# An empty place between the choice of the one-hot clusters and their turning

## The chip, the cores and the metric

The kernel runs on one core of a Trainium2 chip. The metric is the device time of one execution in microseconds. TensorE (PE) multiplies and transposes, VectorE (DVE), ScalarE (ACT) and GpSimd (POOL) do the elementwise work, SyncE (SP) issues most transfers. The four compute engines each run their own instruction stream and meet at semaphores.

## The reference, cut to what matters

```python
q_assign = argmax(einsum('bhsd,hcd->bhsc', q_n, c_n), -1)   # 16 clusters
k_assign = argmax(einsum('bhsd,hcd->bhsc', k_n, c_n), -1)
mask = q_assign[:, :, :, None] == k_assign[:, :, None, :]
scores = where(mask, 0.125 * q @ k.T, -1e9)
x = softmax(scores) @ v          # batch 4, 8 heads, 768 tokens, width 64
# then: 3072 tokens x 512, the best of 8 experts for each token
out[token] = gate * (relu(x[token] @ w1[e]) @ w2[e])        # 512 -> 1024 -> 512
```

Everything is float32. A query attends only to the keys that chose the same of 16 clusters. The change lies in the attention part.

## The kernel before

**Pairs and units.** The work of attention is cut into 16 pairs: a pair is a batch and two neighbouring heads, whose two widths of 64 fill 128 partitions. Inside a pair there are two halves of the queries (384 each), and for each half six blocks of 128 keys. A block for a half is a unit; six units make a group, and a pair has twelve units in two groups. Each unit has three steps. `scores` (L329) multiplies on TensorE: first the one-hot clusters `kH` and `qH` (bf16), which add a large bonus where the clusters match, then `kT` and `qT` into the same PSUM tile `s_ps`. `expo` (L345) takes the exponential on ScalarE into `prob`. `attend` (L350) multiplies `v` with `prob` on TensorE and adds `prob` up in `acc` on VectorE. When a group has ended, `total` (L379) sums `acc` over the keys on TensorE and ScalarE copies it to `den`; `divide` (L394) takes the reciprocal of `den` on VectorE (L400) and multiplies it with the result into `xT` (L401); `rows` (L411) turns `xT` back on TensorE and ScalarE copies it to `xr`.

**Preparation.** While pair n runs, pair n+1 is prepared in nine pieces (`prep_pieces`, L209): three pieces turn q and k (`turn`), `products` multiplies them with the cluster centres, `assign` turns the products and marks the maxima (`sel`), which GpSimd weights (L258), `choose` (L260) makes the one-hot tile `oh` from them on VectorE (L264, L265), `turn_hot(0, "q")` turns the query half of `oh` with six transposes on TensorE (L277) and VectorE copies it to `qH` (L283), `turn_hot(1, "k")` does the same for the keys and ScalarE copies it to `kH` (L285), and `mean` makes a small column `ev` (L298, L306) that `divide` reads. The pieces are kept in the list `prepare`.

**Order.** TensorE, VectorE and ScalarE run the order in which the program is written (`manual_schedule`). The loop at L517 takes two units per turn, so a pair has six turns, here called turn 0 to turn 5. A turn writes, in this order: `scores` and `expo` of the two units that come next, a first piece of preparation, `rows` of the group before (in turns 2 and 5), `attend` of the two present units, `total` and `divide` of the group before (in turns 0 and 3), a second piece of preparation, and a piece of routing if there is one. So a pair has twelve places for pieces, of which nine were used: `assign` and `choose` had the two places of turn 2, the two `turn_hot` those of turn 3, and `mean` the first of turn 4. Fifteen pairs prepare another one; pair 0 itself is prepared ahead of the loop.

**Routing.** After each batch of four pairs, five routing pieces (`route_pieces`, L428) are taken one per turn, from turn 3 of the following pair on: in pairs 4, 8 and 12 `products` (L440) comes in turn 3 and `logits` in turn 4, and in pairs 5, 9 and 13 `choose` (L470) comes in turn 1, with two ScalarE table loads.

**PSUM for the small pieces.** Every preparation piece, `total`, `rows` and the routing pieces take their PSUM tile from `misc()` (L114). Its pool has two buffers, which are handed out by turns:

```python
psM = at.enter_context(tc.tile_pool(name="psM", bufs=2, space=PSUM))
def misc():
    return psM.tile([P, 512], F32, tag="misc", name="misc")
```

The one-hot tiles `oh` (two, L169), `qH` and `kH` (two each) alternate from pair to pair. `prob` has five buffers, `s_ps` two.

Of the kernel before, what the change touches and what calls it, by code (L numbers as in the profile page):

```python
# [35 lines left out]
def kernel(  # L36
# [67 lines left out]
    with ExitStack() as at:  # L104
# [9 lines left out]
        def misc():  # L114
            return psM.tile([P, 512], F32, tag="misc", name="misc")
# [4 lines left out]
        def load(n):  # L120
            b, hp = pairs[n]
            t = ld[n] = {}
            for nm, src in (("q", q), ("k", k), ("v", v)):
                t[nm] = ldp.tile([P, NJ, 2, D], F32, tag=nm + "32", name=nm + "32")
                for h in range(2):
                    nc.sync.dma_start(
                        out=t[nm][:, :, h],
                        in_=src[b, 2 * hp + h].rearrange("(p j) d -> p j d", j=NJ),
                    )
# [79 lines left out]
        def prep_pieces(n):  # L209
# [62 lines left out]
            def turn_hot(i, nm):  # L272
                hot = t[nm + "H"] = trp.tile([P, S], BF16, tag=nm + "H", name=nm + "H")
                bk = misc().bitcast(BF16)
                for j in range(NJ):
                    half, u = divmod(j, NJ // 2)
                    nc.tensor.transpose(  # L277
                        bk[:, P * j : P * j + P],
                        oh[:, u, 2 * i + half].rearrange("p h c -> p (h c)"),
                        identb,  # L280
                    )
                if nm == "q":
                    nc.vector.tensor_scalar(hot, bk[:, 0:S], BIG, None, ALU.mult)  # L283
                else:
                    nc.scalar.copy(hot, bk[:, 0:S])  # L285
# [10 lines left out]
            def mean():  # L296
# [16 lines left out]
                products,  # L313
                assign,
                choose,
                lambda: turn_hot(0, "q"),
                lambda: turn_hot(1, "k"),
                mean,
# [10 lines left out]
        def scores(i):  # L329

            n, hq, j = units[i]
            t = ld[n]
            s_ps = un[i]["s_ps"] = psS.tile([P, 2, 512], F32, tag="s_ps", name="s_ps")
            for l, r, first in (("kH", "qH", True), ("kT", "qT", False)):
                for h in range(2):
                    rows = slice(D * h, D * h + D)
                    nc.tensor.matmul(  # L337
                        s_ps[:, h, 0:HS],
                        lhsT=t[l][rows, P * j : P * j + P],
                        rhs=t[r][rows, HS * hq : HS * hq + HS],  # L340
                        start=first,
                        stop=not first,
                    )

        def expo(i):  # L345
            d = un[i]
            d["prob"] = pp.tile([P, 2, HS], F32, tag="prob", name="prob", bufs=5)
            nc.scalar.activation(d["prob"], d["s_ps"][:, :, 0:HS], ACTF.Exp)  # L348

        def attend(i):  # L350

            n, hq, j = units[i]
            d, g = un[i], gr[i // GU]
            if j == 0:
                g["o_ps"] = psO.tile([P, 512], F32, tag="o_ps", name="o_ps")
            for h in range(2):
                nc.tensor.matmul(  # L357
                    g["o_ps"][D * h : D * h + D, 0:HS],
                    lhsT=ld[n]["v"][:, j, h],
                    rhs=d["prob"][:, h],  # L360
                    start=(j == 0),
                    stop=(j == NJ - 1),
                )
            if j == 1:
                g["acc"] = pp.tile([P, 2, HS], F32, tag="acc", name="acc")
                nc.vector.scalar_tensor_tensor(
                    out=g["acc"],
                    in0=un[i - 1]["prob"],
                    scalar=NJ * EPS,
                    in1=d["prob"],  # L370
                    op0=ALU.add,
                    op1=ALU.add,
                )
                un[i - 1].clear()
            elif j > 1:
                nc.vector.tensor_tensor(g["acc"], g["acc"], d["prob"], ALU.add)  # L376
                d.clear()

        def total(g):  # L379

            d = gr[g]
            bk = misc()
            for h in range(2):
                nc.tensor.matmul(  # L384
                    bk[D * h : D * h + D, 0:HS],
                    lhsT=ones,
                    rhs=d["acc"][:, h],
                    start=True,
                    stop=True,
                )  # L390
            d["den"] = smp.tile([P, HS], F32, tag="den", name="den")
            nc.scalar.copy(d["den"], bk[:, 0:HS])  # L392

        def divide(g):  # L394
            n, hq, _ = units[GU * g]
            b, hp = pairs[n]
            d = gr[g]
            if (b, hq) not in xT:
                xT[b, hq] = xp.tile([P, NHP, HS], F32, tag="xT", name="xT", bufs=3)
            nc.vector.reciprocal(d["den"], d["den"])  # L400
            nc.vector.scalar_tensor_tensor(  # L401
                out=xT[b, hq][:, hp],
                in0=d["o_ps"][:, 0:HS],
                scalar=ld[n]["ev"],
                in1=d["den"],
                op0=ALU.add,
                op1=ALU.mult,
            )
            d.clear()

        def rows(g):  # L411

            n, hq, _ = units[GU * g]
            b, hp = pairs[n]
            U = NJ // 2
            bk = misc()
            for u in range(U):
                nc.tensor.transpose(  # L418
                    bk[:, P * u : P * u + P], xT[b, hq][:, hp, P * u : P * u + P], ident
                )  # L420
            if b not in xr:
                xr[b] = xp.tile([P, NJ, XW], F32, tag="xr", name="xr")
            nc.scalar.copy(
                xr[b][:, U * hq : U * hq + U, P * hp : P * hp + P],
                bk[:, 0:HS].rearrange("p (u w) -> p u w", w=P),
            )
# [78 lines left out]


        prepare, routing = [], []
        with tc.manual_schedule(engines={EngineType.PE, EngineType.DVE, EngineType.Activation}):
            for piece in prep_pieces(0):
                if piece:  # L510
                    piece()
            for m in range(2):
                scores(m)
                expo(m)


            for i in range(0, len(units) + 6, 2):  # L517
                g, part = divmod(i, GU)
                if i < len(units) and i % (2 * NJ) == 0:
                    n = i // (2 * NJ)  # L520
                    assert not prepare
                    if n + 1 < len(pairs):
                        load(n + 1)
                        prepare = prep_pieces(n + 1)
                    if n == 1:

                        for w in range(2):
                            nc.sync.dma_start(
                                out=w1s[w], in_=moe_w1[0].rearrange("(c p) f -> p c f", p=P)
                            )  # L530
                            nc.sync.dma_start(
                                out=w2s[w], in_=moe_w2[0].rearrange("(c p) d -> p c d", p=P)
                            )
                for m in range(i + 2, min(i + 4, len(units))):
                    scores(m)
                    expo(m)
                if prepare:
                    prepare.pop(0)()
                if part == 4 and g > 0:
                    rows(g - 1)  # L540
                for m in range(i, min(i + 2, len(units))):
                    attend(m)
                if part == 0 and g > 0:
                    total(g - 1)
                    divide(g - 1)
                if prepare:
                    prepare.pop(0)()
                if routing:
                    routing.pop(0)()
                if part == 4 and g > 0 and g % (2 * NHP) == 0:  # L550
                    assert not routing
                    routing = route_pieces(g // (2 * NHP) - 1)
            for piece in routing:
                piece()
# [250 lines left out]
```

## Time and profile before

| | |
|---|---|
| median of 3 runs | 924.09 us (923.74 to 926.51) |
| the profiled execution's own time | 926.38 us |
| its span, first to last instruction | 924.4 us |
| busy in the span: PE, DVE, ACT, POOL | 847.7, 358.7, 302.8, 127.9 us |
| mean granted TensorE clock | 0.966 of full speed |

Times in the profile count from the start of the span. The attention part lasts to about 480 us, the routing to about 500 us, and the experts take the rest. A line of the timeline gives the start, the duration, the engine, the line of the kernel, the operation, the output tile and its inputs, and how many instructions were merged; in brackets stands how long the engine sat idle before it and what ended that. The ends of matmuls are modelled, so the distance from one start to the next is the better measure of what a step on TensorE costs. In the rows by stretch the engines stand in the order PE, PEld (the weight loads), DVE, ACT, POOL, each with its number of instructions.

### The profile page before, as it was taken

The page shows a single profiled execution, that of the slowest core. Times are in us where ns is not written, and L with a number is a line of the kernel's source. Part 1 is how long each engine was busy: PE and PEld are TensorE (multiplying, and loading weights), DVE is VectorE, ACT ScalarE, POOL GpSimd, SP SyncE. Part 2 cuts the span into 40 slices and gives each one's busy share as a digit, 9 for nine tenths or more (in the row PEclk, how much of TensorE's full clock was granted, in tenths as well). Part 3 has the DMA queues.
Part 4 walks back from the last instruction along what each step waited for, and adds up shares of the span by engine and source line. Part 5 has one row for each costly group of instructions (what it writes and reads, how often), then busy time and mean ns, then how long its engine had stood idle before and what let it go on. Part 6 is the DMA issues. An engine that isn't in the chain of part 4 may idle for free.

```text
span 924.4 us, 12733 instructions
## 1 busy us (share of the span) xinstructions
PE 847.7 (92%) x5207; PEld 497.6 (54%) x5207; DVE 358.7 (39%) x488; ACT 302.8 (33%) x485; POOL 127.9 (14%) x171
## 2 busy tenths in 40 slices
PE   4999999899998999989943999999999999999996
PEld 2444444344444444434413777676776767677672
DVE  3577676777767777676754000000000000000000
ACT  3445555545455455555540111111111111111110
POOL 4011010211111110111003001111010111101010
PEclk8999999999998999999965999999999999999998
DMA  9822211322203222010002173374746566514610
GB/s 245 291 53 52 52 34 34 106 52 52 49 21 103 52 52 52 19 69 18 1 0 103 41 275 135 122 301 146 283 171 257 200 227 243 199 36 166 256 35 20
DMA packets 105645, 106.85 MB, mean 116 GB/s; under 512 B 77157, under 2 KB 77157, under 8 KB 105072
## 3 DMA queue, kind: packets, MB, share of 16 engines
q1 hardware_dynamic: 100928, 92.30, 31.0%
q0 software_dynamic: 4480, 13.65, 3.9%
q8 instruction: 43, 0.70, 0.3%
q14 instruction: 18, 0.15, 0.0%
q10 hardware_dynamic: 176, 0.05, 0.0%
HBM read 152.11 MB, written 13.64 MB: 179 GB/s over the span
## 4 chain that ended last, share of the span: by engine, by line
PE 39%; issue 28%; DMA 19%; DVE 10%; ACT 2%; POOL 1%; SPq 0%; POOLq 0%; DVEq 0%
DMA out_dram<-y,sidx 18%; PE s_ps L337 15%; PE o_ps L357 13%; DVE acc L376 4%; PE misc L220 3%; PE misc L384 2%; PE misc L235 2%; PE misc L277 2%; DVE oh L265 1%; PE misc L418 1%; DVE sel L257 1%; DVE amax L256 1%; PE misc L440 1%; DVE pm L264 1%; PE misc L248 1%
## 5 line engine op out<-in xcount | busy, mean ns | idle before, releaser
L709 PEld LDWEIGHTS h_ps<-xTm,w1s 128*128 128x128 f32 x1792 | 204.2, 193 | 21.4 <-DVE xTm L699 19.0
L709 PE MATMUL h_ps<-xTm,w1s 128*128 128x128 f32 x1792 | 208.2, 277 | 2.3 <-DMA w1s<-in_moe_w_dram 2.3
L722 PE MATMUL y_ps<-w2s,hT 128*128 128x512 f32 x448 | 201.2, 592 | 0.0
L348 ACT ACTIVATE prob<-s_ps 128x768 f32<-128x768 f32 x192 | 153.4, 811 | 89.9 <-PE s_ps L337 67.7
L699 DVE COPY xTm<-x_ps 128x512 f32<-128x512 f32 x28 | 19.4, 691 | 379.7 <-PE x_ps L697 379.7
L337 PE MATMUL s_ps<-qT,kT 64*128 64x384 f32 x768 | 157.6, 489 | 0.0
L357 PE MATMUL o_ps<-prob,v 128*64 128x384 f32 x768 | 148.9, 510 | 0.0
L376 DVE TENSOR_TENSOR acc<-acc,prob 128x768 f32<-128x768 f32 x128 | 130.2, 1017 | 5.8
L722 PEld LDWEIGHTS y_ps<-w2s,hT 128*128 128x128 f32 x448 | 81.0, 190 | 81.3 <-issue 81.3
L716 ACT ACTIVATE hT<-h_ps 128x512 f32<-128x512 f32 x56 | 33.4, 597 | 242.5 <-PE h_ps L709 242.5
L400 DVE RECIPROCAL den<-den 128x384 f32<-128x384 f32 x32 | 81.7, 2553 | 46.8 <-ACT den L392 46.8
L337 PEld LDWEIGHTS s_ps<-qT,kT 64*128 64x128 f32 x768 | 70.1, 192 | 21.8 <-issue 21.7
L731 POOL DMA_INDIRECT out_dram<-y,sidx x28 | 28.4, 1015 | 355.0 <-ACT y L730 355.0
L357 PEld LDWEIGHTS o_ps<-prob,v 128*64 128x64 f32 x768 | 47.3, 138 | 50.3 <-issue 48.7
L337 PE MATMUL s_ps<-qH,kH 64*128 64x384 bf16 x384 | 64.5, 332 | 1.3 <-ACT prob L348 1.3
L730 ACT ACTIVATE y<-y_ps,xin 128x512 f32<-128x512 f32 x28 | 19.2, 687 | 136.1 <-PE y_ps L722 129.9
L291 POOL TENSOR_TENSOR vs<-v 128x384 f32<-128x384 f32 x16 | 17.4, 1086 | 242.5 <-DMA v<-in_v_dram 242.5
L337 PEld LDWEIGHTS <-kH 64*128 64x128 bf16 x384 | 19.4, 94 | 58.2 <-issue 44.2
L392 ACT COPY den<-misc 128x384 f32<-128x384 f32 x32 | 15.3, 479 | 85.8 <-PE misc L384 85.8
L277 PE MATMUL misc<-identb,oh 128*128 128x128 bf16 x192 | 16.9, 227 | 27.2 <-DVE oh L265 27.2
L258 POOL TENSOR_TENSOR sel<-sel,prefc 128x384 bf16<-128x384 bf16 x16 | 24.2, 1513 | 103.6 <-DVE sel L257 103.6
L229 DVE COPY kT<-misc 128x384 f32<-128x384 f32 x32 | 17.7, 553 | 51.4 <-PE misc L220 51.4
(146 smaller groups left out, 525.0 us busy)
## 6 DMA issues: line engine op xcount, KB each, us to landing
w1s<-in_moe_w_dram SPq DMA_DIRECT2D x30, 2048.0 KB
w2s<-in_moe_w_dram SPq DMA_DIRECT2D x30, 2048.0 KB
x_rows<-xr SPq DMA_DIRECT2D x4, 1539.0 KB
q<-in_q_dram SPq DMA_DIRECT2D x32, 192.0 KB
k<-in_k_dram SPq DMA_DIRECT2D x32, 192.0 KB
v<-in_v_dram SPq DMA_DIRECT2D x32, 192.0 KB
xin<-x_rows,gidx POOLq DMA_INDIRECT x28, 6.9
out_dram<-y,sidx POOLq DMA_INDIRECT x28, 6.7
```

What stands on the lines that cost most here:

```text
L220: nc.tensor.transpose(bk[:, P * j : P * j + P], t[nm][:, NJ // 2 * half + j].rearrange("p h d -> p (h d)"), ident,)
L258: nc.gpsimd.tensor_tensor(sel, sel, bc(prefc, shp, 1), ALU.mult)
L277: nc.tensor.transpose(bk[:, P * j : P * j + P], oh[:, u, 2 * i + half].rearrange("p h c -> p (h c)"), identb,)
L337: nc.tensor.matmul(s_ps[:, h, 0:HS], lhsT=t[l][rows, P * j : P * j + P], rhs=t[r][rows, HS * hq : HS * hq + HS], start=first, stop=not first,)
L348: nc.scalar.activation(d["prob"], d["s_ps"][:, :, 0:HS], ACTF.Exp)
L357: nc.tensor.matmul(g["o_ps"][D * h : D * h + D, 0:HS], lhsT=ld[n]["v"][:, j, h], rhs=d["prob"][:, h], start=(j == 0), stop=(j == NJ - 1),)
L376: nc.vector.tensor_tensor(g["acc"], g["acc"], d["prob"], ALU.add)
L400: nc.vector.reciprocal(d["den"], d["den"])
L709: nc.tensor.matmul(bk[:, m : m + P], lhsT=w1s[j % 2][:, c, f0 + m : f0 + m + P], rhs=d["xT"][:, P * c : P * c + P], start=(c == 0), stop=( ...
L716: nc.scalar.activation(d["hT"][:, f0 : f0 + 512], bk, ACTF.Relu)
L722: nc.tensor.matmul(bk, lhsT=d["hT"][:, P * c : P * c + P], rhs=w2s[j % 2][:, c], start=(c == 0), stop=(c == KF - 1),)
L731: nc.gpsimd.indirect_dma_start(out=out[:], out_offset=bass.IndirectOffsetOnAxis(ap=sidx[:, j : j + 1], axis=0), in_=y, in_offset=None, bou ...
```

## The change

The list of pieces gets a `None` between `choose` and `turn_hot(0, "q")`, and the loop takes pieces with a helper that does nothing for `None`. So turn 3 has nothing in its first place and `turn_hot(0, "q")` in its second, after `total` and `divide`; turn 4 has `turn_hot(1, "k")` in its first place and `mean` in its second, after `attend`. Ten of the twelve places are now taken, one of them by the empty entry. No instruction is added or removed, and the preparation of pair 0 ahead of the loop is as it was.

```diff
@@ prep_pieces
                 products,
                 assign,
                 choose,
+                None,
                 lambda: turn_hot(0, "q"),
                 lambda: turn_hot(1, "k"),
                 mean,
@@ the loop
         prepare, routing = [], []
+
+        def prep():
+            piece = prepare.pop(0) if prepare else None
+            if piece:
+                piece()
+
...
-                if prepare:
-                    prepare.pop(0)()
+                prep()
                 if part == 4 and g > 0:
                     rows(g - 1)
...
-                if prepare:
-                    prepare.pop(0)()
+                prep()
```

## Rows read from the trace of the kernel before

**Rows 1.** By stretch: length, busy us of five engines, granted clock, DMA share, GB/s.

```profile
107.00:134.00 27.00, 25.74 (x175) 12.02 (x173) 19.93 (x23) 13.45 (x20) 3.46 (x4) 1.00 0.20 45
...
180.00:182.00 2.00, 2.00 (x8) 0.71 (x6) 0.57 (x1) 0.00 (x0) 0.00 (x0) 0.50 0.00 0
```

**Rows 2.** Waits from 20 to 440 us: waiter, releaser, total us, times, longest.

```profile
PE misc L277 <- DVE oh L265: 23.5, 15, 2.7
```

**Rows 3.** Timeline of PE, pair 3, from turn 3 to the start of turn 5.

```profile
117.16 0.34 PE L337 MATMUL s_ps<-qH,kH 64*128 64x384 bf16 x2
...
120.21 0.51 PE L277 MATMUL misc<-identb,oh 128*128 128x128 bf16 x6 [1.26 <-DVE oh L265]
120.65 1.51 PE L357 MATMUL o_ps<-prob,v 128*64 128x384 f32 x8
121.99 0.81 PE L384 MATMUL misc<-acc,ones 128*64 128x384 f32 x4
122.73 0.51 PE L277 MATMUL misc<-identb,oh 128*128 128x128 bf16 x6
...
124.89 0.38 PE L298 MATMUL misc<-epsc,vs 128*128 128x1 f32 x2
125.21 1.51 PE L357 MATMUL o_ps<-prob,v 128*64 128x384 f32 x8
126.65 0.34 PE L337 MATMUL s_ps<-qH,kH 64*128 64x384 bf16 x2
```

**Rows 4.** Timeline of DVE in the same stretch.

```profile
119.59 0.56 DVE L265 TENSOR_TENSOR oh<-sel,pm 128x384 bf16<-128x384 bf16 x1
120.75 0.56 DVE L283 TENSOR_SCALAR qH<-misc 128x768 bf16<-128x768 bf16 x1 [0.60 <-PE misc L277]
121.23 0.95 DVE L366 SCALAR_TENSOR_TENSOR acc<-prob 128x768 f32<-128x768 f32 x1
123.36 2.55 DVE L400 RECIPROCAL den<-den 128x384 f32<-128x384 f32 x1 [1.18 <-ACT den L392]
125.95 0.62 DVE L401 SCALAR_TENSOR_TENSOR xT<-o_ps,ev,den 128x384 f32<-128x384 f32 x1
126.48 0.15 DVE L306 COPY ev<-misc 128x1 f32<-128x1 f32 x1
```

**Rows 5.** Timeline of ACT in the same stretch.

```profile
122.85 0.48 ACT L392 COPY den<-misc 128x384 f32<-128x384 f32 x1 [3.04 <-PE misc L384]
123.28 0.80 ACT L285 COPY kH<-misc 128x768 bf16<-128x768 bf16 x1
124.21 1.62 ACT L348 ACTIVATE prob<-s_ps 128x768 f32<-128x768 f32 x2
```

**Rows 6.** Timeline of PE, the preparation of pair 0 ahead of the loop.

```profile
18.90 0.56 PE L298 MATMUL misc<-epsc,vs 128*128 128x1 f32 x2 [0.37 <-DVE qH L283]
```

**Rows 7.** Timeline of PE, pair 0.

```profile
39.73 0.51 PE L277 MATMUL misc<-identb,oh 128*128 128x128 bf16 x6 [1.58 <-DVE oh L265]
```

**Rows 8.** Timeline of PE, pair 4, turns 3 to 5.

```profile
148.81 0.81 PE L384 MATMUL misc<-acc,ones 128*64 128x384 f32 x4
...
153.02 1.51 PE L357 MATMUL o_ps<-prob,v 128*64 128x384 f32 x8
...
154.94 0.34 PE L337 MATMUL s_ps<-qH,kH 64*128 64x384 bf16 x2
```

**Rows 9.** Timeline of PE, pair 5, turns 3 to 5.

```profile
178.49 0.62 PE L277 MATMUL misc<-identb,oh 128*128 128x128 bf16 x6 [2.71 <-DVE oh L265]
...
186.57 0.34 PE L337 MATMUL s_ps<-qH,kH 64*128 64x384 bf16 x2
```

**Rows 10.** Timeline of DVE, pair 5, turn 3.

```profile
177.88 0.56 DVE L265 TENSOR_TENSOR oh<-sel,pm 128x384 bf16<-128x384 bf16 x1
```

**Rows 11.** Timeline of PE, pair 9, turns 3 to 5.

```profile
292.06 0.82 PE L277 MATMUL misc<-identb,oh 128*128 128x128 bf16 x6 [2.71 <-DVE oh L265]
...
301.36 0.34 PE L337 MATMUL s_ps<-qH,kH 64*128 64x384 bf16 x2
```

## The prediction

> **What bounds the kernel now.** I read the stretches first: in 27 us of the attention part, about one pair, TensorE is busy for 25.74 us, VectorE for 19.93, ScalarE for 13.45, and the granted clock is 1.00, the higher of its two levels, 2.4 GHz [rows 1]. So TensorE sets the pace there, and only what leaves it idle can be won without cutting work. Then I read the waits: the only long one of TensorE in the loop is `turn_hot` (L277) on `oh`, 23.5 us over 15 pairs, 2.7 at most [rows 2]. The third view is the timeline of turn 3: the scores start at 117.16, and turning the query half starts at 120.21 after 1.26 us of idle time [rows 3], just after VectorE has written `oh` (119.59 + 0.56 = 120.15) [rows 4]; semaphore and start cost 0.06. The scores of a turn occupy TensorE for 1.72: in turn 4 they stand with the key turning between 122.73 and 124.89, that is 2.16, of which the turning takes 0.44, as that of the queries does (120.21 to 120.65) [rows 3]. So turn 3 could have gone on at 117.16 + 1.72 = 118.88 and lost 1.33.
>
> **The change part by part.** Nothing is added or removed. Three pieces move: twelve transposes on TensorE with the copy to `qH` on VectorE and the copy to `kH` on ScalarE, and `mean` with its copy to `ev`. None of them issues a transfer or anything on GpSimd or SyncE, so no step moves past those queues, and the loads stay where they are in program order.
>
> *What is won.* `attend` and `total` of turn 3 need no `oh`. After the change they follow the scores: attend at 118.88, total 1.34 later (120.65 to 121.99) [rows 3], at T = 120.22. Its other operand, `acc`, is complete: VectorE works in program order and adds it up before `oh`, which is done by 120.15 [rows 4]. The query turning comes 0.74 after total (121.99 to 122.73) [rows 3], at T + 0.74 = 120.96, and `oh` is long there. The wait on `oh` is gone.
>
> *What is late next.* `qH` now stands on VectorE behind `divide`. Before, the copy to `den` starts 0.86 after total (121.99 to 122.85) [rows 3, 5], the reciprocal 1.37 after it (123.36), `xT` 2.59 later (125.95), and the next instruction 0.53 after that (126.48) [rows 4]. The `acc` step before them (0.95 from about 120.2) does not hold them up. So `qH` starts at T + 4.49, takes 0.56 [rows 4], and can release TensorE at T + 5.05 + 0.06 = T + 5.11. Who needs it? The `misc` tiles alternate: in turn 3 and 4 total has one buffer, the query turning the other, the key turning that of total, and `mean` that of the query turning, which is free only when `qH` has been copied. That such a wait is real is seen ahead of the loop, where `mean` comes two tiles after the query turning as well and waits for `qH` [rows 6]. Without it, `mean` would start at T + 0.74 + 0.44 (query turning) + 1.72 (scores) + 0.44 (key turning) + 1.44 (attend, 125.21 to 126.65 [rows 3]) = T + 4.78. So a new wait of 0.33 takes part of the place of the old one of 1.33. With `mean` itself (124.89 to 125.21, 0.32) the scores of turn 5 start at T + 5.43 = 125.65, where they stood at 126.65 [rows 3]: **1.00 us for a usual pair.** Queued behind the waiting `mean` are just these scores, and they, the first of the next pair, need `qH` too, which is there by then.
>
> *What is hidden.* `kH` moves behind the two exponentials of turn 4. They end 1.04 + 1.62 after the scores start (123.17, that is 122.73 + 0.44, to 124.21, and 1.62 [rows 3, 5]), so at T + 1.18 + 2.66 = T + 3.84; the key turning ends at about T + 3.4, and the copy of 0.80 [rows 5] at T + 4.7, 0.7 before the scores that need it. If ScalarE were later by more than that, the excess would be paid in full. `ev` is read only in the next pair. The `acc` steps of turn 4 follow `qH` on VectorE and start earlier than they did (125.3 against 126.5, behind `ev` [rows 4]), so `prob` is freed no later.
>
> *Pair 0* waited 1.58 where the others waited 1.26 [rows 3, 7]: 0.32 more, 1.32.
>
> *Pairs 4, 8, 12.* Routing's `products` takes a `misc` tile after the query turning, so the alternation shifts by one: now the key turning gets the query turning's buffer and waits for `qH`, until T + 5.11, with 0.44 (key turning), 0.32 (`mean`) and 1.92 (attend with `logits`, 153.02 to 154.94) after it: turn 5 at T + 7.79. Before it came 6.13 after total (148.81 to 154.94) [rows 8], and that total came 1.33 + 0.44 = 1.77 after T: T + 7.90. These three win 0.11 each: a wait of the old size returns one turn later.
>
> *Pairs 5, 9, 13.* Routing's `choose` makes VectorE late, TensorE sits idle for 2.71, and then works at clock 0.50, the lower level, 1.2 GHz [rows 1, 9]. Attend and total (2.08) fit into that idle time, so the query turning still starts when `oh` is ready, 178.49 in pair 5. From it, VectorE goes on from 177.88 + 0.58 (`acc`, by the pitch of such an instruction) + 0.95 = 179.41 with the reciprocal, + 2.59 + 0.53 + 0.56 to 183.09; `mean` at 183.15, turn 5 at 183.47, 4.98 after the query turning. It was 8.08 (178.49 to 186.57) [rows 9, 10] and in pair 9 it was 9.30 (292.06 to 301.36) [rows 11]; pair 13 repeats pair 5 within 0.05. Won: 3.10 + 4.32 + 3.15 = 10.6. Of this the clock is worth 1.64, 2.86 and 1.69, because a usual pair takes 6.44 for that stretch (120.21 to 126.65) [rows 3]: 6.2 in sum. I take it that it is won: the largest idle time left is one of about 1.3, and in the usual pair the clock stayed at 1.00 through 1.26 [rows 1, 3].
>
> One rule speaks against that last step. The Trainium skill ("TensorE: Matmul & The Clock Gate", section "A second HAM failure mode: psum-queue depth-cycling") tells of a kernel in which short, frequent pauses of TensorE at PSUM buffers made the clock swing between its levels; the new wait for `mean` is such a pause. By that rule the sum would become the third rival's; the trace does not bear it out, since clock 1.00 stands beside a pause of 1.26 in every pair.
>
> **Sum.** 8 usual pairs at 1.00, 1.32 for pair 0, 0.33 for three, 10.6 for three: 20.2 us. The experts' part is left as it is. The profiled execution took 926.38, its span 924.4 and 2.0 around it: 926.38 - 20.2 = 906.2. That execution lies 2.3 above the median of the runs (924.09), from which the same sum gives 903.9. The clock losses differ from pair to pair (1.64 and 2.86), so part of the 2.3 may be among what is won and part not; I predict 905.0, between the two.
>
> **The rivals.**
> - *The lower clock stays in the three `choose` pairs*, because the waits that are left there (for `acc`, `oh` and then `qH`) do together what the 2.71 did. Then 6.2 is not won: 14.0, 910.1 to 912.4. For it: I know the clock only after 1.26 and after 2.71, not between. Against it: two stretches of work lie between those waits.
> - *The key turning waits for `qH` in all pairs*, as in pairs 4, 8 and 12. Then turn 5 starts at T + 5.11 + 0.44 + 1.44 + 0.32 = T + 7.31 against T + 6.43 before: 0.88 lost in 8 pairs, 0.56 in pair 0, while the `choose` pairs win 1.88 less each, 4.9: in sum 2.4 slower, 926.5 to 928.8. For it: it is what I find in three pairs. Against it: the tiles alternate strictly by the code, and rows 6 fit.
> - *Slower: the clock falls after the new wait.* A fall costs what it cost in pairs 5 and 9, 1.64 to 2.86. In nine pairs that is 15 to 26, and the 6.2 are not won either: 925 to 938. It decides from 20.2 / 15 = 1.35 us for a pair. Against it: the clock of 1.00 through the longer old wait [rows 1].
> - *More is won*: the wait of `mean` isn't there, or the key turning's in the three pairs isn't (0.33 in nine pairs, 0.6 in three and 1.33 in three: 8.8), 895 to 903. Against it: rows 6.
> - *Nothing happens*, if the streams were reordered after being written: 924 to 926. Against it: the timeline keeps the written order on all three engines.
>
> **How the numbers follow.** The forecast (902 to 909) has a chance of 0.77, the clock that stays down in three pairs 0.11, more won 0.05, the key turning everywhere 0.03, nothing 0.02, the falling clock 0.02. About 0.3%, 2.8 us, is what a measurement of this kernel can tell from no change. Faster by more: 0.77 + 0.11 + 0.05 = 0.93; within: 0.04, from the key turning and from nothing; slower: 0.03, the falling clock and the upper part of the key turning. The range reaches from 900, into the case of more, to 912, over most of the clock that stays.
>
> **What would show it.** In the profile of the changed kernel L277 should no longer wait for `oh` except some tenths in pairs 5, 9 and 13; `mean` (L298) should wait for `qH` (L283), some 0.33 in a usual pair; L277's second call should wait 1.3 in pairs 4, 8 and 12; a usual pair should take 25.8 instead of 26.8 us; and the clock should read 1.00 in pairs 5, 9 and 13. The prediction is wrong if `qH` comes later than T + 5.05, if `kH` becomes the last to arrive, or if the clock drops below 1.00 in the loop.

## The result and the profile after

The changed kernel took 903.86 us (median of 4 runs, 903.61 to 904.4), the kernel before 924.32 in the same measurement; the ratio is 0.9775, with a 95% interval of 0.9758 to 0.9792. It is faster by 20.5 us. The profiled execution took 904.4, its span 902.4; against the profiled execution of before, both numbers are 22.0 lower. The lines of the kernel behind the helper have moved by one to five: L338 is L337 of before, L358 is L357, L385 is L384.

The waits of the changed kernel, from 20 to 440 us (waiter, releaser, total us, times, longest), in which the 23.5 us of [rows 2] are gone and 5.2 us have come in another place:

```profile
PE misc L298 <- DVE qH L283: 5.2, 12, 0.5
```

The timeline of TensorE in pair 3, from turn 3 to the start of the next pair (compare [rows 3]):

```profile
114.24 0.34 PE L338 MATMUL s_ps<-qH,kH 64*128 64x384 bf16 x2
...
115.96 1.51 PE L358 MATMUL o_ps<-prob,v 128*64 128x384 f32 x8
117.30 0.82 PE L385 MATMUL misc<-acc,ones 128*64 128x384 f32 x4
118.05 0.51 PE L277 MATMUL misc<-identb,oh 128*128 128x128 bf16 x6
118.49 0.34 PE L338 MATMUL s_ps<-qH,kH 64*128 64x384 bf16 x2
...
120.21 0.51 PE L277 MATMUL misc<-identb,oh 128*128 128x128 bf16 x6
120.65 1.51 PE L358 MATMUL o_ps<-prob,v 128*64 128x384 f32 x8
122.57 0.35 PE L298 MATMUL misc<-epsc,vs 128*128 128x1 f32 x2 [0.41 <-DVE qH L283]
122.85 0.34 PE L338 MATMUL s_ps<-qH,kH 64*128 64x384 bf16 x2
...
126.49 0.34 PE L338 MATMUL s_ps<-qH,kH 64*128 64x384 bf16 x2
```

Turn 3 starts at 114.24 and turn 5 at 122.85, 8.61 later; before it was 9.49 (117.16 to 126.65 in [rows 3]). The query turning at 118.05 no longer waits, and `mean` at 122.57 does, by 0.41. The pair as a whole, from 100.55 to 126.49, takes 25.94 where it took 26.83 (103.46 to 130.29 in the trace of before).

The timeline of VectorE in the same turns (compare [rows 4]):

```profile
118.67 2.55 DVE L401 RECIPROCAL den<-den 128x384 f32<-128x384 f32 x1 [0.58 <-ACT den L393]
121.34 0.62 DVE L402 SCALAR_TENSOR_TENSOR xT<-o_ps,ev,den 128x384 f32<-128x384 f32 x1
121.87 0.55 DVE L283 TENSOR_SCALAR qH<-misc 128x768 bf16<-128x768 bf16 x1
```

`qH` stands directly behind `divide`, starts 4.57 after total and ends 5.12 after it (122.42); `mean` starts 0.15 after that end.

The timelines of TensorE and VectorE in pair 4, turns 3 to 5 (compare [rows 8]), one fence for each engine:

```profile
147.14 0.51 PE L277 MATMUL misc<-identb,oh 128*128 128x128 bf16 x6
147.58 1.51 PE L358 MATMUL o_ps<-prob,v 128*64 128x384 f32 x8
149.02 0.38 PE L298 MATMUL misc<-epsc,vs 128*128 128x1 f32 x2
```

```profile
147.82 0.55 DVE L283 TENSOR_SCALAR qH<-misc 128x768 bf16<-128x768 bf16 x1
```

The key turning starts at 147.14, before the copy to `qH` has even begun, so it doesn't use the query turning's buffer. In this pair the two `misc` buffers are not handed out by turns, as the section on the kernel before said they are. No wait is left here: the pair takes 27.66 instead of 29.07.

The timeline of TensorE in pair 5, turns 3 to 5 (compare [rows 9]), and the stretch of the whole pair (length, busy us of PE, PEld, DVE, ACT, POOL, granted clock, DMA share, GB/s):

```profile
172.32 0.87 PE L385 MATMUL misc<-acc,ones 128*64 128x384 f32 x4 [0.31 <-DVE acc L377]
173.28 0.51 PE L277 MATMUL misc<-identb,oh 128*128 128x128 bf16 x6
...
177.90 0.35 PE L298 MATMUL misc<-epsc,vs 128*128 128x1 f32 x2 [0.50 <-DVE qH L283]
178.18 0.34 PE L338 MATMUL s_ps<-qH,kH 64*128 64x384 bf16 x2
```

```profile
154.00:182.00 28.00, 26.56 (x182) 12.36 (x179) 21.91 (x35) 18.27 (x31) 4.97 (x10) 1.00 0.33 101
```

The idle time of 2.71 has been cut into 0.31 and 0.50 with work between them, and the clock reads 1.00 over the whole pair, as it does in the stretches of pairs 9 and 13:

```profile
261.00:289.00 28.00, 26.56 (x182) 12.17 (x174) 21.92 (x35) 18.28 (x31) 4.99 (x10) 1.00 0.33 100
368.60:396.30 27.70, 26.25 (x179) 12.18 (x176) 21.93 (x35) 18.28 (x31) 5.15 (x10) 1.00 0.20 72
```

In pair 5 the stretch from the query turning to turn 5 takes 4.90 (before 8.08).

By groups of pairs, from the starts of their turns in the two traces: pair 0 won 1.19 (from its turn 3 to its turn 5, because its start differs from execution to execution), the eight usual pairs 0.88 each (7.0), pairs 4, 8 and 12 1.42 each (4.3), and pairs 5, 9 and 13 3.18, 4.38 and 3.22 (10.8). That is 23.2, the distance between the starts of pair 15 (445.46 and 422.25). The span won 22.0, so the part from there to the end is 1.2 longer. That is no more than scatter: in the ten traces of this document this part takes between 478.6 and 481.1, and in the two of the kernel before, 478.9 and 479.6.

### The profile page after: what moved, and what is told of

Its sections match the earlier page's. It is cut to its first block, busy times and chain, and to the rows that moved or that the text cites. A ratio compares the mean times of both kernels' runs of the same rounds, so it can differ in the third digit from the quotient of the medians.

```text
span 902.4 us, 12774 instructions
## 1 busy us (share of the span) xinstructions
PE 842.1 (93%) x5207; PEld 495.4 (55%) x5207; DVE 357.1 (40%) x488; ACT 301.6 (33%) x485; POOL 127.8 (14%) x171
## 4 chain that ended last, share of the span: by engine, by line
PE 38%; issue 28%; DMA 20%; DVE 9%; ACT 2%; POOL 1%; SPq 0%; POOLq 0%; DVEq 0%
DMA out_dram<-y,sidx 19%; PE s_ps L338 15%; PE o_ps L358 12%; DVE den L401 4%; PE misc L220 3%; PE misc L385 2%; PE misc L235 2%; PE misc L419 1%; DVE acc L377 1%; DVE xT L402 1%; ACT den L393 1%; PE misc L441 1%; PE misc L248 1%; DVE qH L283 1%; PE misc L298 1%
## 5 line engine op out<-in xcount | busy, mean ns | idle before, releaser
L338 PE MATMUL s_ps<-qT,kT 64*128 64x384 f32 x768 | 156.3, 486 | 0.0
L358 PE MATMUL o_ps<-prob,v 128*64 128x384 f32 x768 | 145.1, 499 | 0.0
L338 PEld LDWEIGHTS s_ps<-qT,kT 64*128 64x128 f32 x768 | 69.3, 190 | 21.3 <-issue 21.3
L358 PEld LDWEIGHTS o_ps<-prob,v 128*64 128x64 f32 x768 | 46.5, 136 | 56.7 <-issue 55.1
L338 PE MATMUL s_ps<-qH,kH 64*128 64x384 bf16 x384 | 63.9, 329 | 1.6 <-ACT prob L349 1.3
L338 PEld LDWEIGHTS <-kH 64*128 64x128 bf16 x384 | 19.4, 94 | 51.7 <-issue 37.0
L674 POOL DMA_INDIRECT xin<-x_rows,gidx x28 | 29.0, 1035 | 12.3 <-issue 8.2
```

Source lines behind the costliest of these rows:

```text
L338: nc.tensor.matmul(s_ps[:, h, 0:HS], lhsT=t[l][rows, P * j : P * j + P], rhs=t[r][rows, HS * hq : HS * hq + HS], start=first, stop=not first,)
L358: nc.tensor.matmul(g["o_ps"][D * h : D * h + D, 0:HS], lhsT=ld[n]["v"][:, j, h], rhs=d["prob"][:, h], start=(j == 0), stop=(j == NJ - 1),)
L674: nc.gpsimd.indirect_dma_start(out=xin, out_offset=None, in_=x_rows[:], in_offset=bass.IndirectOffsetOnAxis(ap=gidx[:, j : j + 1], axis=0) ...
```

## The experiments

Each starts from the changed kernel unless it says otherwise. The ratios are to the kernel before, on the same chip: its median was 923.87 for the first four runs and 922.24 for the rest.

**Is it the buffer of `mean`, or `qH` itself, that is late?** `mean` is put into the empty place.

```diff
-                None,
+                mean,
                 lambda: turn_hot(0, "q"),
                 lambda: turn_hot(1, "k"),
-                mean,
```

> From the changed kernel, mean is put into the empty place (turn 3, first place) and the place behind attend in turn 4 stays empty. Theory: what is late is qH itself, because VectorE copies it behind divide; the wait goes to whoever needs qH next. Then mean waits for nothing, the scores of turn 5 wait about 0.4 us for qH, a usual pair stays at 25.95 us, and the time stays at 904 us (ratio to the kernel before 0.978). Rival: only the PSUM buffer that mean shares with the query turning costs something; then 0.41 us in each of 12 pairs are won, 899 us (ratio 0.973).

Measured: 902.58 us, ratio 0.9771 (0.9755 to 0.9787), a usual pair 25.90. The timeline of TensorE in pair 3 of this kernel, at the start of turn 5:

```profile
123.20 0.34 PE L337 MATMUL s_ps<-qH,kH 64*128 64x384 bf16 x2 [0.33 <-DVE qH L283]
```

`mean` starts without a wait, in turn 3:

```profile
116.36 0.38 PE L298 MATMUL misc<-epsc,vs 128*128 128x1 f32 x2
```

The wait went on to the scores, the next to need `qH`. The theory holds: a late `qH` is paid for by whoever meets it first, and a free buffer for `mean` alone buys nothing that can be measured.

**`qH` ahead of `divide`.** The query turning goes between `attend` and `total` in turn 3.

```diff
+                if part == 0 and g % 2 == 1:
+                    prep()
                 if part == 0 and g > 0:
                     total(g - 1)
                     divide(g - 1)
-                prep()
+                if not (part == 0 and g % 2 == 1):
+                    prep()
```

> From the changed kernel, the query turning goes between attend and total in turn 3, so that VectorE copies qH ahead of the reciprocal. Theory (qH late behind divide): no piece of turn 4 or the scores of turn 5 wait for qH, a usual pair takes 25.5 instead of 25.95 us; the three pairs with routing's choose wait for oh again, about 1.3 us, and lose some tenths; in sum 9 x 0.41 won and under 1 lost, 900 to 901 us (ratio 0.974 to 0.975). Rival: the wait of mean is set by something else than divide, as the queue of VectorE as a whole; then it stays and the time is 904 us.

Measured: 902.53, ratio 0.9765 (0.9749 to 0.9781), within the measurement of the changed kernel and not the 900 to 901 that were expected. The timeline of TensorE in pair 3 of this kernel:

```profile
116.44 1.51 PE L358 MATMUL o_ps<-prob,v 128*64 128x384 f32 x8
...
119.12 0.34 PE L338 MATMUL s_ps<-qH,kH 64*128 64x384 bf16 x2
...
122.72 0.38 PE L298 MATMUL misc<-epsc,vs 128*128 128x1 f32 x2
123.04 0.34 PE L338 MATMUL s_ps<-qH,kH 64*128 64x384 bf16 x2
```

The wait for `qH` is gone from all pairs, as expected, but a usual pair takes 25.65 and not 25.5: attend, query turning and total, in this order, take 2.68 from the start of attend to the next scores (116.44 to 119.12), where attend, total and query turning take 2.53 (115.96 to 118.49 in the changed kernel). Pairs 5, 9 and 13 wait 1.28 for `oh` again and take 27.93 instead of 27.68. The mechanism is right, but 8 x 0.30 won and 3 x 0.25 lost leave too little to be measured.

**Who copies `qH`.** The copy is given to ScalarE.

```diff
                 if nm == "q":
-                    nc.vector.tensor_scalar(hot, bk[:, 0:S], BIG, None, ALU.mult)
+                    nc.scalar.activation(hot, bk[:, 0:S], ACTF.Copy, scale=BIG)
```

> From the changed kernel, the copy to qH is made by ScalarE (Copy with the scale 2^60) instead of VectorE; ScalarE is idle there between den and the exponentials of turn 4. Theory (qH is late only because VectorE has divide ahead of it): mean no longer waits, 0.4 us less in each of 12 pairs, a usual pair takes 25.5 us, the three choose pairs 27.2; 4 to 5 us below the changed kernel, ratio to the kernel before 0.973. If instead the exponentials, which stand behind the copy on ScalarE, come late by its 0.8 us and the scores wait for their buffer, the gain is lost and the ratio is 0.978 or more.

Measured: 898.57, ratio 0.9729 (0.9699 to 0.9759). The stretch of one pair of this kernel, and ScalarE's timeline at the copy:

```profile
106.00:133.00 27.00, 27.00 (x182) 12.50 (x180) 20.71 (x22) 15.64 (x23) 3.58 (x5) 1.00 0.23 53
```

```profile
117.48 0.48 ACT L393 COPY den<-misc 128x384 f32<-128x384 f32 x1 [1.27 <-PE misc L385]
117.91 0.81 ACT L283 ACTIVATE qH<-misc 128x768 bf16<-128x768 bf16 x1
118.84 1.62 ACT L349 ACTIVATE prob<-s_ps 128x768 f32<-128x768 f32 x2
```

The copy of 0.81 fits between `den` and the exponentials, which start 1.03 after the scores of the turn (117.81) and so no later than in the kernel before (1.04). TensorE is busy for the whole 27 us; a usual pair takes 25.50 and the pairs with `choose` take 27.13, while pairs 4, 8 and 12, which had no wait, stay at 27.66. This version is faster than the kernel before. It was not measured beside the changed kernel: the intervals of the two ratios just touch, and that it is the faster of the two is read from the pairs of its trace, of which the usual ones are 0.45 and those with `choose` 0.55 shorter.

**How the two buffers are handed out.** They get a tag each, and `misc()` takes them strictly in turn.

```diff
-        psM = at.enter_context(tc.tile_pool(name="psM", bufs=2, space=PSUM))
+        psM = at.enter_context(tc.tile_pool(name="psM", bufs=1, space=PSUM))
+        turn_of = [0]
         def misc():
-            return psM.tile([P, 512], F32, tag="misc", name="misc")
+            turn_of[0] ^= 1
+            return psM.tile([P, 512], F32, tag=f"misc{turn_of[0]}", name="misc")
```

> From the changed kernel, the two misc buffers are handed out strictly by turns (two tags with one buffer each) instead of by the pool. Theory: in pairs 4, 8 and 12 the prediction's wait of the key turning for qH was missing only because the pool gave it the other buffer; then the wait of about 1.2 us appears at L277 in these three pairs, they take 28.9 instead of 27.66 us, and the time is 3 x 1.2 higher, 907 to 908 us (ratio 0.982). Rival: the buffers already alternate, and the wait was missing because qH was early enough; then nothing changes, 904 us (ratio 0.978).

Measured: 908.7, ratio 0.9838 (0.982 to 0.9856), a little above the 907 to 908 that were expected. The timeline of TensorE in pair 4 of this kernel, at the key turning:

```profile
148.39 0.49 PE L279 MATMUL misc<-identb,oh 128*128 128x128 bf16 x6 [1.21 <-DVE qH L285]
```

Pairs 4, 8 and 12 take 28.92 instead of 27.66, all others but pair 0, which holds the start, the same within 0.02. So the prediction's wait is real once the buffers alternate. In the changed kernel they don't in these three pairs: the query turning's buffer is still in use there, and the key turning has the other one, that of routing's `products`. By what rule the pool chooses stays open. It is not simply the buffer that comes free first: in the usual pairs, whose time is the same with strict alternation, `mean` waits for the query turning's buffer until the copy to `qH` ends (122.42 in pair 3 of the changed kernel), although that of the key turning is free when ScalarE has copied `kH`, at 121.82. ScalarE's timeline there:

```profile
121.03 0.79 ACT L285 COPY kH<-misc 128x768 bf16<-128x768 bf16 x1
```

**One empty place more.**

```diff
                 choose,
                 None,
+                None,
                 lambda: turn_hot(0, "q"),
```

> From the changed kernel, a second empty place: the query turning moves to the first place of turn 4, the key turning behind attend of turn 4, mean to turn 5. Theory: the wait of mean for qH goes (qH comes right after divide), but now the key turning is the last piece before the scores of turn 5, which wait for the copy to kH, about 0.8 to 0.9 us; a usual pair takes about 0.2 to 0.4 more than 25.95 us, and the time is 906 to 909 us (ratio 0.981 to 0.984). If more room only helps, it is 904 us or less.

Measured: 909.08, ratio 0.9844 (0.9814 to 0.9873), a usual pair 26.36. The timelines of ScalarE and TensorE in pair 3 of this kernel, at the start of turn 5:

```profile
124.22 0.80 ACT L285 COPY kH<-misc 128x768 bf16<-128x768 bf16 x1 [1.50 <-PE misc L277]
```

```profile
125.08 0.34 PE L339 MATMUL s_ps<-qH,kH 64*128 64x384 bf16 x2 [0.89 <-ACT kH L285]
```

Now `kH` is the last to arrive: its copy follows the key turning directly, with nothing between it and the scores. The wait for `mean` is gone, the new one is twice as long. The slack of 0.7 that the prediction gave `kH` lasts for one place, not for two.

**Which pairs bring what.** The empty place only in the preparation that runs in pairs 5, 9 and 13, and its complement.

```diff
-                None,
+                *([None] if n in (6, 10, 14) else []),
```

> The empty place stands only in the preparation that runs in pairs 5, 9 and 13, which routing's choose makes late. Theory: these three pairs alone bring 3.2 to 4.4 us each, idle time and lower clock together, 10.8 in the profile, and the other twelve pairs keep 26.83 (29.07 in 4, 8, 12): 913 to 914 us (ratio 0.988). The clock reads 1.00 in the three pairs. Rival: the clock falls in these pairs whatever the wait; then only some 1.4 us each are won, 919 to 920 us (ratio 0.995), and the clock reads 0.50 for some us in each.

> The complement of the run with the empty place in pairs 5, 9 and 13 only: it stands in the other twelve. Theory: parts add up; the twelve pairs win 0.88 to 1.42 each, 12.4 in the profile, and pairs 5, 9 and 13 keep their wait of 2.71 and their half clock: 911.5 us (ratio 0.9865), and the two runs together win what the change wins. If the time lost to the lower clock hangs on more than these three pairs, the two do not add up by some us.

Measured: 917.46, ratio 0.993 (0.9914 to 0.9945), for the three pairs alone, and 910.58, ratio 0.9864 (0.9837 to 0.9892), for the other twelve. The first missed its 913 to 914: in its trace the three pairs take 27.68, 27.67 and 27.68, at clock 1.00, just as expected:

```profile
160.19:187.87 27.68, 26.23 (x179) 12.17 (x176) 21.91 (x35) 18.27 (x31) 5.10 (x10) 1.00 0.33 101
270.60:298.27 27.67, 26.23 (x178) 12.16 (x175) 21.92 (x35) 18.26 (x31) 5.12 (x10) 1.00 0.33 100
381.02:408.70 27.68, 26.23 (x178) 12.17 (x175) 21.91 (x35) 18.27 (x31) 5.13 (x10) 1.00 0.20 72
```

But the kernel before doesn't lose 10.8 there in each execution. 6.4 us were won (0.7%), and 4.6 of them are the idle time (1.53 in each pair, 29.21 to 27.68); so the clock was worth about 1.8 on the average of the runs and not 6.2; this is an estimate from these numbers, with a margin of some 1.4. That the loss differs from pair to pair shows in the complement, where these pairs keep their wait. Its stretches of pairs 5, 9 and 13:

```profile
154.62:183.83 29.21, 25.97 (x179) 12.24 (x176) 21.75 (x35) 18.34 (x31) 5.13 (x10) 1.00 0.32 97
263.38:292.58 29.20, 25.97 (x178) 12.23 (x176) 21.75 (x35) 18.34 (x31) 5.14 (x10) 1.00 0.31 96
372.13:402.73 30.60, 27.36 (x178) 12.82 (x175) 21.74 (x35) 18.34 (x31) 5.19 (x10) 0.94 0.18 65
```

All three waited 2.71, but only in the third did the clock fall, and it is longer by 1.4. The parts add up within what the measurements can tell: 0.7% and 1.36%, each with an interval of 0.15 to 0.3 to either side, make 2.06%, against 2.25% (2.08 to 2.42) for the whole.

**A second profile of the kernel before.**

> The kernel before, unchanged, for a second profile of it: the first profiled execution took 2.3 us more than the median. Theory: the three choose pairs lose another amount to the clock in each execution (1.64, 2.86 and 1.69 in the first), so that here the sum of pairs 5, 9 and 13 lies 1 to 4 us below the first one's 93.8, and all other pairs take the same within 0.1. Rival: the difference lies in the experts' part or ahead of the loop, and the three pairs take the same.

It took 922.35. The timeline of TensorE in pair 5 (compare [rows 9]), two stretches, behind the waits of pairs 5 and 13, and the stretches of the whole pairs 5, 9 and 13:

```profile
178.37 0.51 PE L277 MATMUL misc<-identb,oh 128*128 128x128 bf16 x6 [2.71 <-DVE oh L265]
178.81 1.51 PE L357 MATMUL o_ps<-prob,v 128*64 128x384 f32 x8
```

```profile
178.00:180.00 2.00, 1.63 (x14) 0.96 (x16) 1.40 (x3) 0.00 (x0) 0.00 (x0) 1.00 0.18 72
...
402.00:404.00 2.00, 1.79 (x10) 1.09 (x12) 1.08 (x3) 0.00 (x0) 0.00 (x0) 0.52 0.00 0
```

```profile
159.24:188.45 29.21, 25.97 (x179) 12.23 (x176) 21.76 (x35) 18.36 (x31) 5.19 (x10) 1.00 0.32 96
271.17:300.37 29.20, 25.97 (x178) 12.24 (x175) 21.75 (x35) 18.35 (x31) 5.17 (x10) 1.00 0.31 95
383.09:413.84 30.75, 27.51 (x178) 12.84 (x175) 21.76 (x35) 18.35 (x31) 5.16 (x10) 0.94 0.18 65
```

The first profile of before had, in pair 5 and in the stretches of pairs 5, 9 and 13:

```profile
179.04 2.83 PE L357 MATMUL o_ps<-prob,v 128*64 128x384 f32 x8
```

```profile
159.36:190.21 30.85, 27.61 (x178) 12.72 (x175) 21.76 (x35) 18.35 (x31) 5.08 (x10) 0.94 0.30 91
272.94:305.00 32.06, 28.82 (x178) 13.39 (x176) 22.08 (x35) 18.40 (x31) 5.15 (x10) 0.89 0.28 87
387.73:418.63 30.90, 27.66 (x178) 12.62 (x175) 21.76 (x35) 18.35 (x31) 5.18 (x10) 0.94 0.18 65
```

After the same wait of 2.71 the attend of pair 5 takes 1.51 here, at clock 1.00, and took 2.83 in the first profile, at the lower level. Pairs 5, 9 and 13 take 29.21, 29.20 and 30.75, in sum 89.2 against 93.8 in the first profile: 4.6 less, while the two spans differ by 4.1. All other pairs but pair 0, which holds the start, agree within 0.02. The theory of this run holds; the difference is somewhat larger than the 1 to 4 us that were expected.

## Why the prediction was right

The time, 903.86, lies 1.1 from the forecast, and the forecast's mechanism is what the trace shows: the wait on `oh` is gone, `qH` is late behind `divide`, `mean` waits for it in the usual pairs, `kH` stays hidden, and the clock stays at its upper level in pairs 5, 9 and 13. One of its own signs of being wrong is there by the letter, with little weight: `qH` is done at T + 5.12, which is 0.07 later than T + 5.05. The sum of 20.2 met 22.0 in the profile; its terms:

- *The usual pair: 1.00 foreseen, 0.88 measured.* The mis-sized term is the start of `mean`: T + 5.27 and not T + 5.11 (the idle time before it is 0.41 where 0.33 was foreseen); 0.04 of this comes back, because the next scores follow `mean` after 0.28 and not 0.32. The reciprocal's distance to `xT` is 2.67 where it was 2.59, and from the end of `qH` to `mean` 0.15 pass, not the 0.06 that were taken from `oh` and the query turning. [rows 6] had a copy to `qH` releasing `mean`, and its own end in the trace of before, 18.76, stands 0.14 ahead of the 18.90 there: the nearer case was at hand. Why the reciprocal's distance is 0.08 longer in this order stays open; with `mean` in the empty place it is 2.59 again.
- *Pairs 4, 8, 12: 0.11 foreseen, 1.42 measured.* Here a step failed: "the alternation shifts by one: now the key turning gets the query turning's buffer". In these pairs the buffers don't alternate, and the key turning has the buffer that is not in use. The run with strict alternation has the wait that was foreseen, 1.21, and wins 0.15 in such a pair (28.92 against 29.07); so the arithmetic was right and its premise wrong. The code alone, two buffers under one tag, doesn't say that they alternate. The rival "more is won" had named just this case, at 1.33 for each of the three pairs, and had been given a chance of 0.05.
- *Pairs 5, 9, 13: 10.6 foreseen, 10.8 measured* against the same execution. But 6.2 of it, the clock, belongs to that execution: in the second profile of before the clock cost only 1.5, in pair 13. What is won in every execution is the idle time, about 1.5 for each pair (29.2 against 27.68). Two profiled executions of the same kernel differ by 4.0 (926.38 and 922.35), and these pairs by 4.6. So the prediction was right not to trust the first one's own time alone. That 20.2 meets the 20.5 between the medians is partly luck: by the run with the empty place in these pairs only they bring about 6.4 on the average and not 10.6, and what is missing, some 4.2 by this estimate, is nearly made up by the 3.9 that pairs 4, 8 and 12 bring beyond the forecast.
- *Behind the start of pair 15* nothing was foreseen and 1.2 lost in the profile, which lies within the scatter of that part over the ten traces (478.6 to 481.1).
- *Pair 0*: 1.32 foreseen, 1.19 measured, short by 0.13, as the usual pair is by 0.12.

Together: 20.2 + 3.9 (pairs 4, 8, 12) - 1.1 (usual pairs and pair 0) + 0.2 - 1.2 = 22.0.

Of the rivals, the clock that stays down in the `choose` pairs and the clock that falls at the new wait are out: clock 1.00 stands in all three pairs and over the loop up to the last pair, with 12 waits of 0.41 to 0.51. The Trainium skill's page "TensorE: Matmul & The Clock Gate" (section "A second HAM failure mode: psum-queue depth-cycling") tells of a kernel in which short, frequent pauses at PSUM made the clock swing. Nothing of the kind is seen in this trace, in which a usual pair of some 26 us has one such wait. The key turning that waits in every pair is out too; it waits in none.

## What to carry to other kernels

When a consumer waits for a producer on another engine, moving it behind independent work of its own engine takes the wait away for nothing, but its output now stands behind whatever that work queues on the next engine: follow each moved copy through the queue it lands in, up to the first reader. Here the copy behind a reciprocal of 2.55 us gave back a third of the wait that was won, and giving that copy to an engine with room brought it home. One place was right and two were too many: the slack of the last arrival (`kH`) sets how far a step can move.

## What the runs showed of the hardware

The same idle time of 2.71 us on TensorE was followed by the lower clock level in five of nine cases (three of three in the first profile of before, one of three in the second, one of three with the empty place elsewhere), and the loss was between 1.4 and 2.9 us when it came. In the seven traces without that idle time the clock stayed at 1.00 in all of these pairs, and after the shorter idle times in the loop, up to 1.59 (pair 0 of the run with the empty place in the `choose` pairs only), it did not fall in any trace.

Between these two lies an idle time of 2.09 in the last pair, which all ten traces have. In eight of them the four matmuls behind it take 0.87, as in the changed kernel; in two the clock falls while they run, and they take 1.20 (the second profile of before) and 1.39 (`mean` in the empty place):

```profile
444.70 0.87 PE L385 MATMUL misc<-acc,ones 128*64 128x384 f32 x4 [2.09 <-DVE acc L377]
```

```profile
444.16 1.39 PE L384 MATMUL misc<-acc,ones 128*64 128x384 f32 x4 [2.09 <-DVE acc L376]
```

So a gain read from one profile's slow stretch is a gain of that execution; here the medians showed less of it.
